# Attention, PReLU layer and soft MoE on one core: the reciprocal of `den` spread by DMA, a later hold of the divided rows, larger K and V rings, and a last stage with block transposes and unread products

## Chip, cores and metric

One NeuronCore of a Trainium2 chip. The metric is the device time of one execution in microseconds (us), lower is better.

## What is computed

```python
def phi(x):
    proj = np.einsum('bhsd,df->bhsf', x, w_phi)
    proj = proj - np.max(np.abs(proj), axis=-1, keepdims=True)
    return np.concatenate([np.exp(proj), np.exp(-proj)], axis=-1)
q_p, k_p = (phi(q), phi(k))                      # q, k, v: 8 batches, 8 heads, 576 tokens, 64
kv = np.einsum('bhsf,bhsd->bhfd', k_p, v)
z = np.sum(k_p, axis=2)
num = np.einsum('bhsf,bhfd->bhsd', q_p, kv)
den = np.einsum('bhsf,bhf->bhs', q_p, z)[..., None] + 1e-06
x = num / den                                    # as 4608 tokens x 512
h = x @ w_in                                     # 512 x 2048
x = (np.maximum(h, 0) + alpha * np.minimum(h, 0)) @ w_out
logits = x @ phi                                 # soft MoE: 8 experts x 4 slots
slot_input = softmax_over_tokens(logits).T @ x   # 32 x 512
slot_out[e] = np.maximum(slot_input[e] @ w1[e], 0) @ w2[e]
out = softmax_over_slots(logits) @ slot_out
```

## The kernel before

**Tiling.** The 4608 tokens are cut into 12 blocks of 384 (`n`), and the 2048 hidden features into 16 chunks of 128 (`c`). One pair (n, c) is a slot: `gemm` (line 498 of the kernel before) makes 12 products of 128 x 384 into the bank `ph` (line 505; `x` and `w_in` are each held as a high and a low fp32r part, and the low-by-low term is left out). `leaky` (510) applies the PReLU on ACT and DVE into `gT`, `turn_g` (528) transposes `gT` in 32 x 32 blocks on DVE and makes products for the logits (`pl`, 540), and per block `softmax` (549) weighs the tokens and adds their sum (`pS`, line 602) into `acc`. `w_out` is applied only to that 32-row sum, in the last stage.

**Attention in the same program.** `k_pair` makes `kv` and `z` for a pair of heads, `q_pair` (382) projects, exponentiates and makes `num` (435) and `den` (442) for a pair of heads and one block, and `q_finish` (453) ends a block: `den` has four groups of 32 rows, one for each sign and head of a pair; a product with the constant `densum` adds the two signs and spreads each sum over 16 rows (460), DVE takes the reciprocal (464), ACT and DVE split it into two fp32r parts `rhl` (469, 470), and for each of the four pairs two products with the constant `densel` spread it over 64 rows a head (`sel`, 477 and 478). DVE multiplies `num` with `sel` (484), ACT rounds it to `xhi` (485), and DVE takes the rest `xlo` (486). `xhi` and `xlo` have one buffer each: those of block n can be written when the last `ph` of block n-1 has read its own.

**Order.** Every step is put by hand at a slot and a phase of it (`at(slot, "pre" | "pe" | "pe2" | "post", ...)`), and a timeline scheduler then sets each engine's order; an engine runs its instructions in that order. All DMAs of the kernel go through the one queue of SP, in order, and each waits there for its buffer. Two blocks (`VB`) bring back deferred `gT` from DRAM in `reload`.

**Last stage.** Behind the last `ph` come the softmax of block 11, its `pS`, four adds into `acc`, then transposes and products with `w_out` (`pg` 757, `px` 762), `sT`, the experts' first layer (`pe`, 782) with transposes `pth` on PE (790), the second layer (`pso`, 819), between which nine groups of four transposes `pc` (808) turn the combine weights into `cT`, and then for each half of the 512 columns (`dh`) the output: 36 products `po` (836) of 128 x 256 fp32r, copied out by ACT and DVE (841, 839) into three rotating tiles `os`, and 9 DMAs of 512 KB (842). The weights `w_out`, `w1`, `w2` come by DMA as 144 pieces of 256 KB (`fetch`) into buffers as these fall free. `spin` (105) issues products that nobody reads (`SPIN` says how many at each place).

Of the kernel before, what the change touches and what calls it, by code (L numbers as in the profile page):

```python
# [28 lines left out]
TB = BT // 128  # L29
NT = T // 128  # L30
E = 8
# [3 lines left out]
KVB = 6  # L35
# [8 lines left out]
SPIN = [5, 3, 13, 6]  # L44

F64_LEAST = struct.unpack("<f", struct.pack("<I", 0x38100000))[0]
# [15 lines left out]
def attention_prelu_softmoe(ctx: ExitStack, tc, qT, kT, v, wphi, w_in, w_out, alpha, phi, w1, w2, out):  # L62
# [10 lines left out]
    gT_d = dram.tile([NDEF, NC, 128, BT], F32, name="gT_d")  # L73

# [27 lines left out]
    def spin(count, before):  # L102
        turn = bank("spin", ps_d)
# [28 lines left out]
    eps_den = const.tile([128, 1], F32, name="eps_den")  # L132
    densum = att.tile([128, 128], F32, name="densum")
    densel = xp.tile([128, NP, 128], F32R, tag="densel", name="densel")

    wpr = sm.tile([128, NC, NSL], F32, tag="wpr", name="wpr")
    acc = const.tile([128, 4, 512], F32, name="acc")
# [5 lines left out]
    def setup_a():  # L143
        nc.vector.memset(ones, 1.0)
        nc.vector.memset(eps_den, 0.0)
        nc.vector.memset(eps_den[0:32], 1e-6)
        nc.vector.memset(eps_den[64:96], 1e-6)

    def setup_b():
# [8 lines left out]
        for p in range(NP):  # L158
            for j in range(2):
                a, b = 64 * j + p, 64 * j + 32 + p  # L160
                r = 32 * p + 16 * j
                nc.vector.tensor_tensor(
                    out=densum[:, r:r + 16], in0=ident[:, a:a + 1].to_broadcast([128, 16]),
                    in1=ident[:, b:b + 1].to_broadcast([128, 16]), op=ALU.add)
                nc.vector.tensor_copy(densel[:, p, 64 * j:64 * j + 64], ident[:, r:r + 1].to_broadcast([128, 64]))

    sched = {}

# [14 lines left out]
    def conv(slot, src, use):  # L183
# [21 lines left out]
        def second():  # L205
# [3 lines left out]
            nc.vector.tensor_tensor(out=w, in0=m, in1=st["sign"], op=ALU.mult)  # L209
# [172 lines left out]
    def q_pair(slot, n, p, late=0):  # L382
# [34 lines left out]
        def feature():  # L417
            pj, mb = st["pj"], st["mb"]
            nc.vector.tensor_tensor(out=pj, in0=pj, in1=mb, op=ALU.subtract)  # L419
            tags = ("qa0", "vg0", "qa1", "vg1") if n == 0 else ("qa0",) * 4  # L420
            st["e", 0] = (attk.tile([128, 4, BT], F32, tag=tags[p], name="qe")[:, 0:2] if tags[p][0] == "v"
# [5 lines left out]
        def attend():  # L427
# [25 lines left out]
    def q_finish(slot, n):  # L453
        st = q_st[n]

        def sums():
            rd = st["rd"] = sm.tile([128, BT], F32, tag="dT", name="rd")
            nc.scalar.activation(rd, st["den"][:, 0:BT], AF.Identity, bias=eps_den)
            ps = st["ps"] = bank("densum")
            nc.tensor.matmul(ps[:, 0:BT], densum, rd, start=True, stop=True)  # L460
# [5 lines left out]
        def split():  # L466
            rhl = xp.tile([128, 2, BT], F32R, tag="rhl", name="rhl")
            rhi, rlo = st["rhi"], st["rlo"] = rhl[:, 0], rhl[:, 1]
            nc.scalar.copy(rhi, st["rc"])
            nc.vector.tensor_tensor(out=rlo, in0=st["rc"], in1=rhi, op=ALU.subtract)  # L470
            xhi_t[n] = xp.tile([128, KD, BT], F32R, tag="xhi", name="xhi")
            xlo_t[n] = xp.tile([128, KD, BT], F32R, tag="xlo", name="xlo")

        def spread(p):
            def go():
                ps = st["sel", p] = bank("sel")
                nc.tensor.matmul(ps[:, 0:BT], densel[:, p, :], st["rhi"], start=True, stop=False)  # L477
                nc.tensor.matmul(ps[:, 0:BT], densel[:, p, :], st["rlo"], start=False, stop=True)
            return go

        def scale(p):
            def go():
                xs = st["num"][:, p, :]
                nc.vector.tensor_tensor(out=xs, in0=st["sel", p][:, 0:BT], in1=xs, op=ALU.mult)
# [4 lines left out]
        at(slot, "pe", sums)  # L489
        at(slot, "post", recip)  # L490
        at(slot + 1, "pre", split)
        for p in range(NP):
            at(slot + 1, "post", spread(p))
            at(slot + 1, "post", scale(p))
# [27 lines left out]
    def reload(n, c):  # L522
        gT4 = attk.tile([128, 4, BT], F32, tag=f"vg{c // 4 % 2}", name="gT4")
# [374 lines left out]
```

## Time and profile before

| what | us |
|---|---|
| three runs | 1056.34, 1056.88, 1061.24 (median 1056.88) |
| the profiled execution, its own time | 1057.16 |
| its span, first to last instruction | 1055.4 |
| PE busy / DVE busy / ACT busy / POOL busy | 984.1 / 773.8 / 469.8 / 149.2 |
| DMA: moved, mean rate | 110.60 MB, 105 GB/s |

A busy PE is not PE at its peak: products are pipelined, and their ends are modelled. The engines' shares are means over stages with different limits, so the profile is read by stages: up to about 234 us the conversion of `w_in` and `w_out` and the attention of the first blocks fill DVE, from 259 to 954.5 us `ph` runs without a break, and from 954.5 us on the last stage.

### The profile page before, as it was taken

What the parts mean: (1) busy time and instruction counts of PE and PEld (TensorE: products, weight loads), DVE (VectorE), ACT (ScalarE), POOL (GpSimd) and SP (SyncE); (2) the same over time, 40 slices, a digit from 0 to 9 for tenths busy, and PEclk for the clock granted to TensorE, in tenths of its full rate; (3) what the DMA queues carried; (4) which work ended last, traced back from release to release, by engine and by line L of the source; (5) the groups of instructions that cost most, each with busy time, mean ns of one, the idle gap of its engine ahead of it and who ended that gap; (6) DMA issues with size and microseconds to landing.
All of it is one profiled execution on the core that took longest, in us unless ns stands there. A gap on an engine that the chain in (4) does not pass through costs nothing.

```text
span 1055.4 us, 21864 instructions
## 1 busy us (share of the span) xinstructions
PE 984.1 (93%) x9038; PEld 685.2 (65%) x9038; DVE 773.8 (73%) x1552; ACT 469.8 (45%) x908; POOL 149.2 (14%) x88
## 2 busy tenths in 40 slices
PE   3787998998999999999999999999999999998994
PEld 1445776774676776676666776767667767787353
DVE  3999989879767578587878687687888486874133
ACT  3876867776444245144235344343334343200133
POOL 2201214121111212121112111121112221000000
PEclk7898999998999999999999999999999999999995
DMA  5343653653010111010401111110401200769879
GB/s 199 120 141 125 193 188 114 225 178 100 9 31 31 39 31 38 20 51 19 163 10 38 32 39 31 31 38 19 160 19 46 96 8 2 249 226 327 261 235 309
DMA packets 71986, 110.60 MB, mean 105 GB/s; under 512 B 7248, under 2 KB 47312, under 8 KB 71888
## 3 DMA queue, kind: packets, MB, share of 16 engines
q1 hardware_dynamic: 71888, 109.22, 32.0%
q8 instruction: 71, 1.16, 0.4%
q14 instruction: 27, 0.22, 0.1%
HBM read 89.27 MB, written 19.92 MB: 103 GB/s over the span
## 4 chain that ended last, share of the span: by engine, by line
PE 71%; DVE 3%; DMA 2%; ACT 1%; issue 1%; DVEq 0%; ACTq 0%; SPq 0%
PE ph L505 34%; PE num L435 5%; PE pS L602 5%; PE pkv L333 5%; PE pl L540 4%; PE den L442 3%; PE pq L403 3%; PE pk L289 2%; DMA out_dram<-os 2%; PE pso L819 1%; PE pe L782 1%; PE sel L477 1%; PE pt L355 1%; PE pr L558 1%; PE densum L460 1%; PE pkv L339 1%
## 5 line engine op out<-in xcount | busy, mean ns | idle before, releaser
L505 PE MATMUL ph<-xhi,w 128*128 128x384 f32 x1536 | 435.2, 351 | 6.5 <-DVE gT L515 4.4
L505 PEld LDWEIGHTS ph<-xhi,w 128*128 128x128 f32 x1536 | 279.0, 189 | 76.8 <-issue 41.5
L505 PE MATMUL ph<-xlo,w 128*128 128x384 f32 x768 | 255.1, 340 | 0.0
L415 POOL PARTITION_ALL_REDUCE mb<-pj x48 | 140.4, 2928 | 553.0 <-ACT pj L409 450.1
L505 PEld LDWEIGHTS ph<-xlo,w 128*128 128x128 f32 x768 | 143.6, 188 | 12.6 <-issue 6.1
L515 DVE SCALAR_TENSOR_TENSOR gT<-gT,alpha_neg,ph 128x384 f32<-128x384 f32 x104 | 62.9, 605 | 77.3 <-ACT ph L514 76.5
L532 DVE STREAM_TRANSPOSE gb<-gT 128x384 f32<-128x384 f32 x192 | 105.6, 566 | 5.7 <-DMA gT<-gT_d 1.9
L513 ACT ACTIVATE gT<-ph 128x384 f32<-128x384 f32 x104 | 50.8, 489 | 114.8 <-PE ph L505 114.0
L425 ACT ACTIVATE qe<-pj 128x768 f32<-128x768 f32 x92 | 73.9, 839 | 59.5 <-DVE pj L419 56.2
L517 DVE TENSOR_SCALAR gT<-ph,alpha_sb 128x384 f32<-128x384 f32 x88 | 53.8, 613 | 46.2 <-PE ph L505 45.8
L333 PE MATMUL pkv<-kp,vt 128*64 128x256 f32 (+1 forms) x640 | 85.0, 400 | 1.1 <-DVE wpr L250 1.1
L435 PE MATMUL num<-qe,kv 128*64 128x192 f32 (+1 forms) x496 | 70.9, 417 | 0.0
L283 ACT ACTIVATE kp<-kp 128x512 f32<-128x512 f32 (+1 forms) x80 | 46.8, 586 | 51.6 <-DVE kp L282 51.1
L333 PEld LDWEIGHTS pkv<-kp,vt 128*64 128x64 f32 (+1 forms) x640 | 41.3, 140 | 39.4 <-issue 17.1
L280 DVE TENSOR_REDUCE mx<-pk 128x4 f32<-128x512 f32 (+1 forms) x80 | 50.2, 627 | 11.4 <-PE pk L289 9.7
L602 PE MATMUL pS<-gb,d 32*32 32x256 f32 x2304 | 55.0, 385 | 0.3 <-DVE logits L594 0.2
L403 PE MATMUL pq<-qraw,wp 64*128 64x384 f32 x192 | 48.9, 562 | 6.7 <-DMA qraw<-in_qT_dram 4.1
L446 ACT COPY num<-num 128x384 f32<-128x384 f32 x48 | 22.8, 475 | 67.1 <-PE num L435 64.2
L409 ACT COPY pj<-pq 128x768 f32<-128x768 f32 x44 | 35.2, 799 | 36.3 <-PE pq L403 36.3
L419 DVE TENSOR_TENSOR pj<-pj,mb 128x768 f32<-128x768 f32 x48 | 46.6, 971 | 6.0 <-POOL mb L415 6.0
L282 DVE TENSOR_TENSOR kp<-pk,mx 128x512 f32<-128x512 f32 (+1 forms) x80 | 50.2, 627 | 0.8 <-PE pkv L333 0.2
L514 ACT ACTIVATE ph<-ph 128x384 f32<-128x384 f32 x104 | 50.6, 487 | 0.0
(191 smaller groups left out, 1345.6 us busy)
## 6 DMA issues: line engine op xcount, KB each, us to landing
w<-in_w_dram SPq DMA_DIRECT2D x58, 256.0 KB, 5.7
qraw<-in_qT_dram SPq DMA_DIRECT2D x48, 192.0 KB, 2.4
out_dram<-os SPq DMA_DIRECT2D x18, 512.0 KB, 3.7
raw<-in_w_in_dram SPq DMA_DIRECT2D x16, 512.0 KB, 3.6
raw<-in_w_out_dram SPq DMA_DIRECT2D x16, 512.0 KB, 4.2
gT_d<-gT SPq DMA_DIRECT2D x32, 192.0 KB, 2.0
gT<-gT_d SPq DMA_DIRECT2D x8, 768.0 KB, 5.2
pf<-in_w_dram SPq DMA_DIRECT2D x21, 256.0 KB, 6.0
```

Source lines behind the costliest of these rows:

```text
L333: return lambda: nc.tensor.matmul(pkv[64 * j:64 * j + 64, 0:256], vt[:, 64 * j:64 * j + 64], feats(t, j).rearrange("p s f -> p (s f)"), st ...
L403: lambda j=j, sl=slice(64 * j, 64 * j + 64): nc.tensor.matmul(pq[j][:, 0:BT], wp[sl], st["qraw"][sl], start=True, stop=True)
L415: nc.gpsimd.partition_all_reduce(mb, pj, 128, bass_isa.ReduceOp.absmax)
L425: nc.scalar.activation(st["e", s], pj, AF.Exp, scale=(1.0, -1.0)[s])
L435: lambda s=s, j=j: nc.tensor.matmul(num[64 * j:64 * j + 64, o:o + w], kvs[:, s, 64 * j:64 * j + 64], st["e", s][:, j, o:o + w], start=(s = ...
L505: gemm_last[0] = nc.tensor.matmul(h, (w_in_hi, w_in_lo)[a][c][:, 128 * k:128 * k + 128], (xhi, xlo)[b][:, k, :], start=(i == 0), stop=(i = ...
L513: nc.scalar.activation(gT, h, AF.Relu, scale=-1.0)
L514: nc.scalar.activation(h, h, AF.Relu)
L515: nc.vector.scalar_tensor_tensor(out=gT, in0=gT, scalar=alpha_neg[:, c:c + 1], in1=h, op0=ALU.mult, op1=ALU.add)
L517: nc.vector.tensor_scalar(out=gT, in0=h, scalar1=0.0, scalar2=alpha_sb[:, c:c + 1], op0=ALU.min, op1=ALU.mult)
L532: nc.vector.transpose(out=gb[n, c // 8][:, c % 8, :], in_=gT)
L602: lambda j=j, i=i, h=h: nc.tensor.matmul(pS[i][32 * (j % 4):32 * (j % 4) + 32, 256 * h:256 * h + 256], st["d"][32 * i:32 * i + 32, 32 * j: ...
```

## The change

- **Reciprocal by DMA.** `den` is laid out so that the two signs add up in the bank (384 columns as two halves of 192 on other rows). DVE adds 1e-6 and takes the reciprocal of 192 columns, two DMAs write it to DRAM (`rc_d`) and two read it back spread over 64 rows each (`bc`, 128 x 4 x 384). `densum`, `densel`, `rhl`, `sel` and their products are gone.
- **Later hold.** The block's end moves to slot 16(n-1)+7, the multiplication with `bc` (`divide`) and the split (`scale`) to six slots later; the multiplication is held on DVE behind the PReLU of that slot (`mark`). The pairs of Q stand 3 slots apart, not 4.
- **Rings.** `KVB`, the buffers of `kv` and `zt`, 6 to 8; `gT` comes back in 2 chunks a DMA with three buffers, not in 4 with two.
- **Last stage.** The sum in `acc` is carried by products (`carry`, `pa`), the four row groups are added in the bank; `pg` is four whole transposes; the experts' hidden rows and the combine weights are transposed in 32 x 32 blocks on DVE, so `pth` and `pc` are gone; `w2` is loaded with another row order; `po` becomes a pair of fp32 products of 32 rows each that use different row groups and banks; behind each pair stand three unread products into `idle`; `os` has nine tiles; more unread products stand between the other steps.

```diff
-KVB = 6
+KVB = 8
-SPIN = [5, 3, 13, 6]
+SPIN = [5, 3, 8, 3, 8, 5, 5, 5, 3]
...
-            for b, o, w in segments(n):
-                kvs, zt = kv_t[NP * b + p]
+            for s in (1, 0):
                 together([
-                    lambda g=g: nc.tensor.matmul(
-                        den[32 * g:32 * g + 32, o:o + w], zt[:, g, :], st["e", g % 2][:, g // 2, o:o + w],
-                        start=(p == 0 and o == 0), stop=(p == NP - 1 and o + w == BT))
-                    for g in (3, 1, 2, 0)])
+                    lambda j=j, h=h, zt=kv_t[NP * ((n * BT + h * HB) // S) + p][1]: nc.tensor.matmul(
+                        den[64 * j + 32 * h:64 * j + 32 * h + 32, 0:HB], zt[:, 2 * j + s, :],
+                        st["e", s][:, j, HB * h:HB * h + HB],
+                        start=(p == 0 and s == 1), stop=(p == NP - 1 and s == 0))
+                    for j in (1, 0) for h in (1, 0)])
...
         def recip():
-            rc = st["rc"] = sm.tile([128, BT], F32, tag="dT", name="rc")
-            nc.vector.reciprocal(out=rc, in_=st["ps"][:, 0:BT])
...
-                nc.tensor.matmul(ps[:, 0:BT], densel[:, p, :], st["rhi"], start=True, stop=False)
-                nc.tensor.matmul(ps[:, 0:BT], densel[:, p, :], st["rlo"], start=False, stop=True)
...
+            rd = sm.tile([128, BT], F32, tag="dT", name="rd")[:, 0:HB]
+            nc.vector.tensor_scalar(out=rd, in0=st["den"][:, 0:HB], scalar1=1e-6, scalar2=None, op0=ALU.add)
+            nc.vector.reciprocal(out=rd, in_=rd)
+            for j in range(2):
+                nc.sync.dma_start(rc_d[n % 2][j].rearrange("p h t -> h p t"), rd[64 * j:64 * j + 64])
+        def widen():
+            bc = st["bc"] = xp.tile([128, NP, BT], F32, tag="bc", name="bc")
+            for j in range(2):
+                nc.sync.dma_start(
+                    bc[64 * j:64 * j + 64], rc_d[n % 2][j, 0:NP].rearrange("p h t -> p (h t)").unsqueeze(0).to_broadcast([64, NP, BT]))
...
+                ins = nc.vector.tensor_tensor(out=xs, in0=st["bc"][:, p, :], in1=xs, op=ALU.mult).ins
+                tc.add_manual_dep(ins, mark[max(k for k in mark if k <= slot + 6)].name, nosync, reason="behind the load")
...
-                q_pair(NC * (n - 1) + 4 * p + -6 + (-1 if n == 1 else 0), n, p)
-        q_finish(-39 + 18 + 5 if n == 0 else NC * (n - 1) + -6 + 12 + 5 + (-1 if n == 1 else 0), n)
+                q_pair(NC * (n - 1) + 3 * p - 6 - (p > 0 or n == 1), n, p)
+        q_finish(-39 + 18 + 5 if n == 0 else NC * (n - 1) + 7, n)
...
+            spun[0] = spin(SPIN[3], together([
+                lambda i=i: nc.tensor.matmul(pa[32 * i:32 * i + 32, :], tsc, acc[i], start=True, stop=False)
+                for i in (3, 2, 1, 0)], spun[0]))
+            gather()
...
+                last[dh] = spin(SPIN[8], together([
+                    lambda j=j, r=2 * h + j, sl=slice(64 * h + 32 * j, 64 * h + 32 * j + 32): nc.tensor.matmul(
+                        po[j][:, 0:256], logits[sl, 4 * i:4 * i + 4, :].rearrange("p t s -> p (t s)"), sor[sl], start=True, stop=True)
+                    for j in range(2)], last.get(dh)), idle)
```

Where the block's end moved, PE's order at the start of block 6 (`w_1268` and `w_1259` hold the last chunk's weights of block 5, `w_637` and `w_633` the first chunk's of block 6). Before:

```order
L289 MATMUL pk<-wp,kraw 128x128 x8
L505 MATMUL ph<-xhi,w_1268 128x384
L477 MATMUL sel<-rhl,densel 128x384 x2
L478 MATMUL sel<-rhl,densel 128x384 x2
L477 MATMUL sel<-rhl,densel 128x384
L478 MATMUL sel<-rhl,densel 128x384
L442 MATMUL den<-qe,zt 32x192 x8
L477 MATMUL sel<-rhl,densel 128x384
L478 MATMUL sel<-rhl,densel 128x384
L505 MATMUL ph<-xhi,w_637 128x384 x4
L540 MATMUL pl<-gT,wpr 32x384 x4
```

And with the change:

```order
L345 MATMUL pt<-ident,kvT 128x128 x3
L492 MATMUL ph<-xhi,w_1259 128x384 x2
L492 MATMUL ph<-xlo,w_1259 128x384
L492 MATMUL ph<-xhi,w_1259 128x384
L393 MATMUL pq<-qraw,wp 128x384 x2
L492 MATMUL ph<-xhi,w_633 128x384 x6
L528 MATMUL pl<-gT,wpr 32x384 x4
L492 MATMUL ph<-xhi,w_662 128x384
```

The eight `sel` products that stood between the two blocks' `ph` are gone, and so is the `den` of the next block among them; a projection `pq` stands there now.

In the last stage, PE around the output (`w_...` hold `w2`). Before:

```order
L825 MATMUL prp<-so,tident 128x256
L819 MATMUL pso<-w_10242,hTm 32x256 x3
L819 MATMUL pso<-w_10245,hTm 32x256 x4
L819 MATMUL pso<-w_10248,hTm 32x256 x4
L819 MATMUL pso<-w_10251,hTm 32x256 x4
L819 MATMUL pso<-w_10254,hTm 32x256 x4
L836 MATMUL po<-sor,cT 128x256 x36
L825 MATMUL prp<-so,tident 128x256
L836 MATMUL po<-sor,cT 128x256 x36
```

And with the change:

```order
L822 MATMUL prp<-so,tident 128x256
L816 MATMUL pso<-num,acc_111 32x256 x3
L816 MATMUL pso<-bc,acc_111 32x256 x6
L816 MATMUL pso<-w_10212,acc_111 32x256 x4
L816 MATMUL pso<-w_10215,acc_112 32x256 x4
L816 MATMUL pso<-w_10218,acc_112 32x256 x3
L834 MATMUL po<-sor,logits 128x256 x2
L108 MATMUL idle<-ident 128x128 x3
```

The last two rows follow one another 18 times; then come the 25 `pso` that are left, `prp`, and again 18 times a pair of `po` and three unread products. The output of the first half so stands ahead of a part of the second half's `pso`.

## Rows read from the trace of the kernel before

**Rows 1.** The page, its first line.

```profile
span 1055.4 us, 21864 instructions
```

**Rows 2.** Windows by stage: us; PE, PEld, DVE, ACT, POOL busy; PEclk; DMA share; GB/s.

```profile
234.00:259.00 25.00, 19.20 (x149) 10.45 (x147) 23.51 (x46) 15.31 (x31) 2.32 (x1) 0.86 0.32 96
...
329.00:954.50 625.50, 617.02 (x5926) 440.45 (x5923) 471.00 (x919) 235.28 (x451) 88.81 (x48) 1.00 0.19 63
954.50:983.00 28.50, 24.16 (x329) 16.98 (x331) 8.82 (x25) 3.81 (x14) 0.95 (x1) 0.88 0.83 270
...
1000.70:1022.80 22.10, 22.10 (x300) 11.92 (x299) 7.46 (x39) 5.78 (x11) 0.00 (x0) 1.00 0.79 251
1022.80:1055.40 32.60, 16.99 (x74) 13.32 (x74) 13.63 (x21) 10.73 (x19) 0.00 (x0) 0.66 0.87 290
```

**Rows 3.** Chain of waits, one stretch of dense `ph` products: start us, length us.

```profile
938.72 8.55 PE ph L505 x48
```

**Rows 4.** Groups of instructions by shape, PE; busy us, mean ns, idle before.

```profile
L477 PE MATMUL sel<-rhl,densel 128*128 128x384 f32 x48 | 18.2, 401 | 8.0 <-DVE num L484 5.6 <-ACT rhl L469 2.4
...
L478 PE MATMUL sel<-rhl,densel 128*128 128x384 f32 x48 | 16.2, 372 | 1.9 <-DVE rhl L470 1.9
...
L460 PE MATMUL densum<-rd,densum 128*128 128x384 f32 x24 | 10.4, 513 | 0.0
```

**Rows 5.** Timeline of PE at the start of block 6; idle before in brackets.

```profile
549.00 0.60 PE L477 MATMUL sel<-rhl,densel 128*128 128x384 f32 x2
549.92 0.62 PE L478 MATMUL sel<-rhl,densel 128*128 128x384 f32 x2 [0.32 <-DVE rhl L470]
552.38 0.69 PE L477 MATMUL sel<-rhl,densel 128*128 128x384 f32 x1 [1.84 <-DVE num L484]
...
553.32 1.51 PE L442 MATMUL den<-qe,zt 128*32 128x192 f32 x16
...
555.57 0.94 PE L505 MATMUL ph<-xhi,w 128*128 128x384 f32 x4
...
557.22 0.45 PE L505 MATMUL ph<-xhi,w 128*128 128x384 f32 x1
```

**Rows 6.** Chain of waits, last stage.

```profile
961.97 3.99 PE pS L602 x173
...
976.30 5.02 PE px L762 x32
...
983.02 1.85 PE pe L782 x16
...
987.41 3.57 PE pe L782 x32
...
1006.05 0.57 PE pso L819 x8
...
1007.21 1.86 PE pso L819 x32
```

**Rows 7.** Timeline, last stage: unread products; output issues; last output copy.

```profile
958.13 3.06 PE L105 MATMUL spin<-ident 128*128 128x128 f32 x26
...
1024.25 26.85 SPq L842 DMA_DIRECT2D out_dram<-os  x18
...
1049.97 0.69 DVE L839 COPY os<-po 128x512 f32<-128x512 f32 x1 [0.95 <-DMA out_dram<-os]
```

**Rows 8.** Timeline of PE, one row-tiled pair and the product behind it.

```profile
541.94 0.92 PE L403 MATMUL pq<-qraw,wp 64*128 64x384 f32 x4
542.78 0.45 PE L505 MATMUL ph<-xhi,w 128*128 128x384 f32 x1
```

**Rows 9.** DMA issues: count, KB each, median us to landing.

```profile
gT_d<-gT SPq DMA_DIRECT2D x32, 192.0 KB, 2.0
...
vt<-in_v_dram SPq DMA_DIRECT2D x16, 320.0 KB, 3.2
```

**Rows 10.** Waits of the DMA queue SP: total us, times, longest.

```profile
SPq L391 <- PE pq L403: 224.4, 33, 22.3
```

More of the change, by code (lines that the diff above doesn't have):

```diff
@@ L73, in attention_prelu_softmoe @@
     gT_d = dram.tile([NDEF, NC, 128, BT], F32, name="gT_d")
+    rc_d = [dram.tile([2, 32, 2, HB], F32, name=f"rc_d{i}") for i in range(2)]
     const = ctx.enter_context(tc.tile_pool(name="const", bufs=1))
@@ L100, in together, with spin @@
         return before
-    def spin(count, before):
-        turn = bank("spin", ps_d)
+    def spin(count, before, turn=None):
+        turn = turn or bank("spin", ps_d)
         return together([
@@ L157, in setup_b @@
             nc.vector.tensor_tensor(out=o, in0=o, in1=ident[:, 96:128], op=ALU.add)
[L158 to L165, printed above, removed]
     sched = {}
+    mark = {}
     after = [NC * (b + 1) + VR for b in VB]
@@ L546, in attention_prelu_softmoe @@
     first = [True]
[L547 removed]
+    gemm_last, spun, last = [None], [None], {}
     def softmax(step, n):
@@ L606, in gather @@
             if n == NB - 1:
-                spun[0] = spin(SPIN[3], last)
+                spun[0] = spin(SPIN[4], end)
         def add():
@@ L715, in attention_prelu_softmoe @@
                 fetch(attk, tag)
-            for tag in ("vg0", "vg1"):
-                fetch(attk, tag, 3)
+            for i in range(3):
+                fetch(attk, "vg", 1, 3)
             for i in range(KPB):
                 fetch(attk, "kp2", 2, KPB)
-        if slot == 170:
+        if slot == 168:
             close_pool("attq")
@@ L772, in attention_prelu_softmoe @@
-    hTm = [attk.tile([128, 4, E, NSL], F32, tag="kp2", name="hTm", bufs=KPB) for f in range(2)]
-    for t in hTm:
-        nc.gpsimd.memset(t, 0.0)
-    hrs = attk.tile([128, 2, 512], F32, tag="kp2", name="hrs", bufs=KPB)
-    hr_t = {}
-    for eg in range(2):
+    pa = last["pa"]
+    spun[0] = spin(SPIN[5], together([
+        lambda i=i: nc.tensor.matmul(pa[32 * i:32 * i + 32, :], tident[:, 0:32], acc[i], start=False, stop=True)
+        for i in range(4)], spun[0]))
+    half = [slice(0, 256), slice(256, 512)]
@@ new lines, in attention_prelu_softmoe @@
+    nc.scalar.copy(acc[0][:, half[0]], pa[:, half[0]])
+    nc.vector.tensor_copy(acc[1][:, half[1]], pa[:, half[1]])
+    pg, px, psi = bank("pg"), bank("px"), bank("psi")
+    spun[0] = spin(SPIN[6], together([
+        lambda c=c: nc.tensor.transpose(pg[:, 128 * c:128 * c + 128], acc[c // 2][:, 128 * c:128 * c + 128], ident)
+        for c in range(4)], spun[0]))
+    nc.scalar.copy(aT[:, half[0]], pg[:, half[0]])
+    nc.vector.tensor_copy(aT[:, half[1]], pg[:, half[1]])
+    spun[0] = spin(SPIN[7], together([
+        lambda i=i, c=c: nc.tensor.matmul(
+            px[32 * c:32 * c + 32, :], aT[:, 128 * c + 32 * i:128 * c + 32 * i + 32], got["wo", 4 * i + c], start=(i == 0), stop=(i == 3))
+        for i in range(4) for c in range(4)], spun[0]))
@@ new lines, in attention_prelu_softmoe @@
+    nc.scalar.activation(acc[2][:, half[0]], px[:, half[0]], AF.Identity, scale=lsum)
+    nc.vector.tensor_scalar(out=acc[3][:, half[1]], in0=px[:, half[1]], scalar1=lsum, scalar2=None, op0=ALU.mult)
+    for k in range(KD):
+        nc.tensor.matmul(psi[:, 32 * k:32 * k + 32], acc[2 + k // 2][:, 128 * k:128 * k + 128], tident[:, 0:32], start=True, stop=True)
+    nc.scalar.copy(sT, psi[:, 0:KD * NSL].rearrange("p (k s) -> p k s", k=KD))
+    own = sm.tile([128, 8], F32, tag="sc", name="own", bufs=2)
@@ new lines, in attention_prelu_softmoe @@
+    for eg in range(2):
+        for j in range(4):
+            nc.vector.tensor_reduce(
+                out=own[:, j:j + 1], in_=ident[:, 36 * j + 16 * eg:36 * j + 16 * eg + 4], axis=AX.X, op=ALU.add)
+        nc.vector.tensor_reduce(out=own[:, 4 + eg:5 + eg], in_=own[:, 0:4], axis=AX.X, op=ALU.add)
+    nc.vector.tensor_scalar(out=own[:, 4:6], in0=own[:, 4:6], scalar1=F32_MOST, scalar2=None, op0=ALU.mult)
+    hT = []
+    for eg in range(2):
+        hr = attk.tile([128, EF], F32, tag="kp2", name="hr", bufs=KPB)
@@ L813, in attention_prelu_softmoe @@
-    so2 = pf.tile([128, 2, 256], F32, tag="pf12", name="so")
-    sor2 = pf.tile([128, 2, 256], F32R, tag="pf13", name="sor")
+            nc.vector.tensor_scalar(
+                out=hr[:, 512 * fh:512 * fh + 512], in0=pe, scalar1=0.0, scalar2=own[:, 4 + eg:5 + eg], op0=ALU.max, op1=ALU.min)
+        t = acc[2 * eg:2 * eg + 2]
+        for b in range(2):
+            nc.vector.transpose(
+                out=t[b].rearrange("p (b s) -> p b s", s=32),
+                in_=hr.rearrange("p (f b) -> p b f", b=32)[:, 16 * b:16 * b + 16])
```

201 lines of the change are left out of this document (79 added, 122 removed).

## The prediction

> **What bounds the kernel now.** I read the page first, then the windows by stage, the groups of PE, the timeline of a block's start, and last the chain of the final stage. The span is 1055.4 us [rows 1]; the profiled execution took 1057.16 us, 1.8 us more, and 0.28 us above the median of the runs. I count from 1057.2.
>
> The windows [rows 2] show three regimes. From 329 to 954.5 us PE is busy 617 of 625.5 us at the full clock (1.00 is 2.4 GHz; a figure below it is a mean over stretches at this level and at 1.2 GHz) while DVE has 471 us of work: PE's order sets the pace, and what leaves PE there leaves the time. Between 234 and 259 us it is otherwise: DVE is busy 23.5 of 25 us, PE 19.2, and the granted clock is 0.86; the `ph` of block 2 have to wait for the end of its attention. In the last stage two things alternate. From 1000.7 to 1022.8 us PE is busy throughout, from 1022.8 us on only 17.0 of 32.6 us, at a clock of 0.66, with the DMA engines at 0.87 and 290 GB/s: there the output's transfers are the bound. Eighteen issues of 512 KB go out in 26.85 us, 1.49 us for one tile [rows 7].
>
> **Reciprocal by DMA, on PE.** For each block eight `sel` and one `densum` product go; the new `den` has as many columns in as many passes as the old, and costs what it cost. A dense `ph`, of the same 128 x 384 fp32r shape as `sel`, takes 8.55 / 48 = 0.178 us [rows 3]; `densum`, fp32, has two records of 0.51 us that overlap in part, 10.4 / 12 = 0.87 us for one block [rows 4]. By pace that is 8 x 0.178 + 0.87 = 2.3 us a block, 25 us for the eleven blocks behind the first. But the products also stand in a chain: PE waited 8.0 us before the first and 1.9 us before the second kind of `sel` [rows 4]. Block 6 is the plainest: from the first `sel` at 549.0 us to the dense `ph` at 557.22 us pass 8.2 us [rows 5], in which `sel` have 1.4 us of work; PE waits 0.32 us for the split and 1.84 us for the multiplication on DVE. The new order has no product that waits for DVE there; a rest stays, since `xhi` has one buffer and its first part is cast on ACT only when the old block's last product has read it. Lower end: pace alone with `densum` at one record, (1.42 + 0.51) x 9 blocks behind 329 us = 17 us. Upper end: all that the groups show, 18.2 + 16.2 + 10.4 + 9.9 = 55 us. I take the pace of eleven blocks and half of the waits, **-30 us**, near the pace, because the busy time of a group holds waits that other products may fill.
>
> **The same on DVE, ACT and SP.** DVE loses half of each reciprocal and the split, and its product with `bc` stays; it has 155 us to spare behind 329 us [rows 2], so this counts nothing there. If it fails to hide, the next to be late is the PReLU, and with it `gT` and PE. New are four DMAs a block on SP. The nearest rows are a write of 192 KB, landed 2.0 us after its issue, and a load of 320 KB in 3.2 us [rows 9]; `bc` is two of 384 KB, so the way there and back takes about 2.0 + 3.5 to 4.5 = 6 us. The order puts the product with `bc` behind the reciprocal by one to eight slots of 12 `ph` (seven of the eleven blocks five or more, block 9 four, block 10 two, blocks 1 and 7 one), and a slot of dense `ph` alone is 2.1 us. In the tight blocks DVE would stand for some 2 us; PE has work for that time, as `xhi` is needed only at the block's end. I count 0; upper end 3 blocks x 4 us = 12 us.
>
> **Block 2 and the rings.** The Q pairs end four slots sooner and the end of a block too; DVE's order now has 25 PReLUs ahead of block 2's reciprocal where it had 32, and its `w_out` conversions come later, beside `ph`. The 25 us from 234 to 259 us hold 19.2 us of PE work at a reduced clock, with DVE full. Ends: nothing is gained (DVE's work remains and must be done before the steady stretch), or all but the 5.8 us that PE idles plus the clock's loss, 25 x 0.14 = 3.5 us, and as much again at the two starts before it: 19 us. I take **-8 us**, near the middle. The larger rings of K and V and the three buffers of `gT` free loads sooner; nothing in the stretch where PE is full waits long for them, so 0.
>
> **The last stage up to the output.** Priced from its own rows [rows 6, 7]. An unread product costs 3.06 / 13 = 0.235 us (26 records are 13 products). A pass of four products of 512 columns side by side is 3.57 / 4 = 0.89 us, from `pe`; one of 256 columns 1.86 / 4 = 0.465 us, from `pso`.
> - From the last `ph` (954.5) to `pS` (961.97): 7.5 us, unchanged.
> - `pa`, one pass, and three unread products: 0.9 + 0.7. Then `pS`, 4.0.
> - Eight unread products, which cover the copies: 1.9. The closing `pa` 0.9, five unread 1.2, four transposes 0.6, five unread 1.2, `px` four passes 3.6 (5.02 before, partly at half clock), five unread 1.2, `psi` and its copy 0.8.
> Sum 24.5: `pe` starts near 979.0 instead of 983.0. `pe` takes 4 x 3.57 = 14.3 without the transposes `pth` and `psi` between, so it ends near 993.3 instead of 1000.7. The 128 `pso` take 14.9, the two `prp` with the copies round them 3.0. That is 11 us gained ahead of the output, and the loads of `w2` keep up: 46 pieces behind `px` at some 0.75 us each (256 KB at the output's rate) end by about 1012 us.
>
> **The output itself.** Here the change works against itself. 36 pairs of `po` come with 108 unread products, in PE's own order, so they are paid whether the output waits for DMA or not. The trace has no fp32 pair of 32 rows by 256 columns. The nearest row is `pq`, a pair of 64 rows and 384 columns between full-array products: the next product begins 0.84 us behind it [rows 8], and 0.84 x 256 / 384 = 0.56 us. With three unread products 0.56 + 0.71 = 1.27 us a pair, 2.5 us a tile, against 1.49 us for its DMA. Thirty-six pairs take 45.7 us. So: 993.3 + 14.9 + 3.0 + 45.7 = 1056.9, less the last three unread products, plus the last copy 0.4 and, as before, 4.7 us from the last copy's end (1050.66) to the span's end: about 1061.3, **+6 us** against 1055.4. Lower end: the unread products cost nothing and DMA bounds the output, 18 x 1.49 = 27 us behind the last load, 1044 us, -11. Upper end: the pair's two products do not run side by side, 36 x 0.465 = 17 us more, +23.
>
> On the price of a pair, rows and a page can be set against each other. A visit of `pso` among transposes, x8, takes 0.57 us where the dense rows give 0.465 [rows 6]: some 0.1 us is lost by going to and fro. The Trainium skill (TensorEngine Tiling (Array Packing), Key Properties) says that a change of the tiling mode drains TensorE; the pairs and the unread full-array products change it 72 times. By that rule, with the trace agreeing in the 0.1 us, the `pq` price holds; without it the dense price would give 36 x (0.465 + 0.71) = 42.3 us, 3.4 less.
>
> **Sum.** -30 - 8 + 6 = -32: 1057.2 - 32 = 1025 us; against the median 0.3 less, which I let stand.
>
> **Rivals.**
> - The output is bounded by DMA after all and the unread products lie in its shadow: -30 - 8 - 11 gives 1008 us. For it speaks that DMA is the bound there now; against it that 2.5 us of PE work a tile exceed 1.49. Chance 0.13.
> - The pairs do not run side by side: 1025 + 17 = 1042 us. The pairs of `pq` do share a pass, which speaks against it. 0.10.
> - PE gets only the pace back, and block 2 nothing, since DVE, at three quarters busy, becomes late instead: 1057.2 - 17 + 6 = 1046 us. 0.13.
> - Slower: the way through DRAM is late. SP is one queue in order, and loads of Q in it waited 33 times, 224.4 us in all, up to 22.3 us [rows 10]. If the read of `bc` stands behind such a wait in each block, DVE stops at the product with `bc`, the PReLU behind it stops, and `ph` finds no free bank. A mean wait of 6.8 us plus 6 us is 13 us; it decides once it exceeds the distance from reciprocal to product, about 2 to 4 us a slot, so in blocks with three slots or fewer. With 5 us lost at each of eleven blocks, and no gain of waits there, 1057.2 - 20 + 55 + 6 - 8 = 1090 us; at half of them about 1063. The order of SP puts at most a few loads between write and read. 0.07.
> - The unread products don't do what they are for: the clock falls in the output all the same (it was 0.66, rows 2), and 45.7 us of products grow by half or more, 1050 to 1070 us. Against it: PE would be busy without a break. 0.05.
>
> **Numbers.** The forecast has 0.52, with 1012 to 1038 us for itself. The range 1003 to 1046 us reaches over the first three rivals and leaves out the last two and the tails, about 0.2. A measurement of this kernel can tell some 0.5%, 5 us, from no change. Faster by more than that: 0.52 + 0.13 + 0.10 and most of 0.13, 0.86; within it, 0.06; slower, 0.08.
>
> **What would show it.** Right: no PE wait at a block's start longer than about 1 us; block 2's first `ph` well before 258 us; `pe` starting 24 to 25 us behind the last `ph`; the output's pairs at about 1.27 us each with PE full, the clock at full speed, and outgoing DMAs 2.5 us apart, with the stage from the last `ph` to the end some 106 us long (101 before). Wrong: `bc` as the reason of DVE's idle time; output DMAs 1.5 us apart; or a body of the blocks, from `ph` to `ph`, as long as before.

## The result, and the profile after

The changed kernel takes 1071.41 us (median of 4 runs, 1070.07 to 1076.39), the one before beside it 1057.89: ratio 1.0131, interval 1.0100 to 1.0162. It is 1.3% slower; 1025 us, 3% faster, was predicted. The profiled execution took 1070.44 us.

The windows of the changed kernel by stage, columns as in [rows 2]; ahead of them the page's first line:

```profile
span 1068.7 us, 22668 instructions
...
329.00:952.70 623.70, 596.11 (x5951) 431.78 (x5952) 461.81 (x902) 220.05 (x427) 84.64 (x43) 0.98 0.25 73
952.70:980.00 27.30, 24.55 (x351) 16.83 (x353) 9.32 (x36) 4.21 (x11) 0.00 (x0) 0.94 0.95 302
...
1005.90:1068.70 62.80, 57.70 (x412) 39.44 (x412) 15.72 (x37) 13.79 (x37) 0.00 (x0) 0.99 0.54 184
```

The first row answers the second of [rows 2]. PE's busy time fell from 617.0 to 596.1 us, as the products that went away promised, but its idle time rose from 625.5 - 617.0 = 8.5 to 27.6 us and the granted clock fell from 1.00 to 0.98: the last `ph` ends at 952.7 instead of 954.5 us. From there to the end it takes 116.0 us instead of 100.9, with the DMA engines half idle in the output (0.54, before 0.87).

The waits of the changed kernel (engine, line and tile, what it waited for: us in all, times, longest):

```profile
DVE num L472 <- DMA bc<-rc_d: 19.5, 4, 6.7
ACT xhi L465 <- DVE num L472: 19.4, 4, 6.8
...
PE pl L528 <- DMA gT<-gT_d: 12.6, 4, 4.0
...
PE ph L492 <- ACT xhi L465: 10.7, 4, 5.9
```

Two waits are new. In four blocks the product of `num` with `bc` stands for the read of `bc`, and PE behind it for `xhi`; and PE waits for the parked rows `gT`. The chain of waits ahead of block 7 shows the first (start us, length us):

```profile
608.85 0.83 PE den L431 x16
...
611.22 1.23 DVE rd L449
...
612.74 0.28 SPq L451
613.02 0.05 issue
613.07 3.40 DMA rc_d<-rd
616.47 0.02 issue
616.49 4.93 DMA bc<-rc_d
...
621.51 1.96 DVE num L472 x4
```

From the first issue to the landing of `bc` pass 621.42 - 612.74 = 8.7 us; I had taken 6. It lands as the last `ph` of block 6 ends (621.4 us); PE has a `pq` and three `pt` left to do there and then waits 1.48 us for `xhi`. The longest wait, 5.9 us, is block 1's.

The chain in the last stage, as in [rows 6]:

```profile
979.95 13.94 PE pe L799 x128
993.89 9.06 PE pso L816 x166
1002.95 0.63 PE prp L822 x2
1003.58 2.30 PE pso L816 x40
1005.87 0.63 PE po L834 x4
1006.50 0.87 PE idle L108 x6
```

The last two rows repeat to the end: a pair 0.63 us, three unread products 0.86, 1.495 us in all, for 36 pairs 53.8 us; 18 output DMAs go out in 56.39 us, 3.1 us apart, where 26.85 us stood before [rows 7].

### The profile page after: what moved, and what is told of

Same layout as the page of the kernel before. It is cut to its first block, busy times and chain, and to the rows that moved or that the text cites. A ratio compares the mean times of both kernels' runs of the same rounds, so it can differ in the third digit from the quotient of the medians.

```text
span 1068.7 us, 22668 instructions
## 1 busy us (share of the span) xinstructions
PE 987.5 (92%) x9428; PEld 698.5 (65%) x9428; DVE 761.6 (71%) x1509; ACT 448.1 (42%) x883; POOL 145.7 (14%) x86
## 4 chain that ended last, share of the span: by engine, by line
PE 73%; DVE 13%; DMA 6%; ACT 4%; issue 3%; SPq 0%; POOL 0%; DVEq 0%; ACTq 0%; POOLq 0%
PE ph L492 34%; PE pkv L323 6%; PE num L425 5%; PE pS L591 4%; PE pl L528 3%; PE den L431 3%; PE idle L108 3%; PE pq L393 3%; PE po L834 2%; PE pk L279 2%; DMA bc<-rc_d 2%; DMA gT<-gT_d 2%; DMA rc_d<-rd 2%; PE pso L816 1%; PE pe L799 1%
## 5 line engine op out<-in xcount | busy, mean ns | idle before, releaser
L492 PE MATMUL ph<-xhi,w 128*128 128x384 f32 x1536 | 435.5, 353 | 20.3 <-ACT xhi L465 10.7
L492 PEld LDWEIGHTS ph<-xhi,w 128*128 128x128 f32 x1536 | 283.1, 192 | 82.9 <-issue 37.7
L492 PE MATMUL ph<-xlo,w 128*128 128x384 f32 x768 | 260.1, 345 | 1.8 <-DVE xlo L466 1.8
L492 PEld LDWEIGHTS ph<-xlo,w 128*128 128x128 f32 x768 | 146.0, 191 | 14.3 <-issue 6.6
L323 PE MATMUL pkv<-kp,vt 128*64 128x256 f32 (+1 forms) x640 | 87.4, 409 | 1.4 <-ACT kp L274 1.4
L270 DVE TENSOR_REDUCE mx<-pk 128x4 f32<-128x512 f32 (+1 forms) x80 | 50.0, 625 | 15.3 <-PE pk L279 12.0
L528 PE MATMUL pl<-gT,wpr 128*32 128x384 f32 x384 | 42.8, 521 | 14.6 <-DMA gT<-gT_d 12.6
L279 PE MATMUL pk<-wp,kraw 64*128 64x128 f32 x512 | 39.4, 296 | 14.1 <-issue 10.5
```

Source lines behind the costliest of these rows:

```text
L279: lambda t=t, j=j, sl=slice(64 * j, 64 * j + 64): nc.tensor.matmul(st["pk"][:, j, F * t:F * t + F], st["kraw"][sl, 128 * t:128 * t + 128], ...
L323: return lambda: nc.tensor.matmul(pkv[64 * j:64 * j + 64, 0:256], vt[:, 64 * j:64 * j + 64], feats(t, j).rearrange("p s f -> p (s f)"), st ...
L492: gemm_last[0] = nc.tensor.matmul(h, (w_in_hi, w_in_lo)[a][c][:, 128 * k:128 * k + 128], (xhi, xlo)[b][:, k, :], start=(i == 0), stop=(i = ...
L528: lambda g=g: nc.tensor.matmul(pl_t[n][32 * g:32 * g + 32, :], wpr[:, c - 3 + g, :], gT_t.pop((n, c - 3 + g)), start=(c == 3), stop=(c == ...
```

## Experiments

Each edit is against the kernel that is named with it; where none is, against the changed one. Where the span went is read from three pieces of each profile, in us: the end of block 2's last `ph`; from there to the last `ph`; from there to the end of the span.

| kernel | median | block 2 ends | then to the last `ph` | then to the end |
|---|---|---|---|---|
| before | 1057.9 | 328.6 | 626.0 | 100.9 |
| changed | 1071.4 | 325.0 | 627.7 | 116.0 |
| tail_alone | 1072.7 | 328.3 | 629.6 | 114.1 |
| front_alone | 1062.8 | 322.4 | 634.9 | 103.7 |
| no_unread | 1045.4 | 323.0 | 628.3 | 91.2 |
| unread1 | 1064.6 | 323.4 | 629.2 | 116.7 |
| tail_no_unread | 1046.5 | 327.2 | 626.2 | 88.7 |
| rc_prev | 1026.1 | 317.6 | 617.6 | 89.7 |
| k_early | 1033.5 | 334.5 | 608.7 | 89.5 |
| k_e3 | 1035.6 | 337.5 | 609.2 | 87.5 |
| kv6 | 1045.6 | 325.2 | 629.3 | 90.9 |
| ring4 | 1038.0 | 324.4 | 621.8 | 90.6 |
| kr6 | 1027.8 | 328.4 | 607.3 | 90.1 |
| spread4 | 1029.3 | 330.5 | 607.4 | 90.2 |
| gt2_act | 1042.3 | 323.7 | 625.2 | 90.9 |
| gt_act | 1026.0 | 330.8 | 602.7 | 90.0 |
| gt_pool | 1033.3 | 330.2 | 609.3 | 92.4 |

### Which half is slow

**tail_alone**: the kernel before with the new last stage.

```diff
-SPIN = [5, 3, 13, 6]
+SPIN = [5, 3, 8, 3, 8, 5, 5, 5, 3]
...
+        if n == NB - 1:
+            at_step(step + 2, "pe2", carry)
```

> The kernel before with the new last stage alone (reciprocal, hold, Q spacing and rings as before). Theory M (the last stage itself costs 15 us: from the last ph to the end 101 us before, 116 us in the changed kernel; what precedes it is another matter): before + 15, about 1073 us. Rival (the last stage is long only because of what the front part hands it, loads or clock): before, 1058 us, or less by the 4 us that pe starts earlier.

Measured 1072.69 us, ratio 1.0134 (1.0103 to 1.0165). **front_alone**: the changed kernel with the old last stage.

```diff
-SPIN = [5, 3, 8, 3, 8, 5, 5, 5, 3]
+SPIN = [5, 3, 13, 6]
...
-            at_step(step + 2, "pe2", carry)
```

> The changed kernel with the old last stage. Theory M (the 25 us of PE work that left are eaten by new waits of PE, 44.7 us idle between the first and the last ph against 19.0): within 3 us of before, 1055 to 1058 us. Rival (the front part is a gain of some 20 us, which the last stage's 15 us and something between them hide): about 1040 us.

Measured 1062.76 us, ratio 1.0044 (1.0024 to 1.0064). So the last stage alone costs the whole loss, and the front, where I looked for 38 us, gives nothing; tail_no_unread and no_unread below, which differ by the front alone, lie 1 us apart.

### The output

**no_unread**: nothing between the pairs.

```diff
-SPIN = [5, 3, 8, 3, 8, 5, 5, 5, 3]
+SPIN = [5, 3, 8, 3, 8, 5, 5, 5, 0]
```

> The changed kernel without the three unread products behind each pair of the output (SPIN's last entry 0). Theory M (they are paid in PE's order, 36 x 0.865 = 31 us, and hold back what DMA could send at 1.5 us a tile): output bounded by DMA from about 1010 us on, 27 us + 5, a span near 1044 us, time near 1047 us, 24 us less than the changed kernel. Rival (without them the clock falls to half and the pairs take 1.2 us or more each): span near 1058 us, time near 1060 us. Second rival (they cost nothing, DMA bounds the output anyway): 1071 us.

Measured 1045.4 us, ratio 0.9875 (0.9850 to 0.9899). The stage shrinks from 116.0 to 91.2 us, and the output is bounded by its DMAs again; the windows, and the queue of SP (17 of the 18 output DMAs, as the row begins at 1010 us; 26.21 / 17 = 1.54 us each):

```profile
1004.90:1029.00 24.10, 21.97 (x179) 11.60 (x177) 11.21 (x30) 9.72 (x30) 0.00 (x0) 1.00 0.92 309
1029.00:1042.40 13.40, 2.91 (x25) 1.68 (x22) 2.70 (x8) 2.22 (x7) 0.00 (x0) 0.72 0.91 302
```

```profile
1009.86 26.21 SPq L839 DMA_DIRECT2D out_dram<-os  x17
```

The clock, which the unread products were to hold, stays at 1.00 through the pairs without them: the last pair ends at 1032.5 us, and the 0.72 of the second window comes from what lies behind it. **unread1**: one in place of three (the last number of `SPIN` is 1).

> The changed kernel with one unread product behind each pair of the output instead of three. If what the three cost is PE's own time, 0.288 us each in the trace of after: 36 pairs take 10 us more than in no_unread, of which the outgoing DMAs hide the part in the first half of the output: 1050 to 1056 us. Rival (one keeps the clock up to the end and costs nothing behind the DMAs): 1043 to 1046 us.

Measured 1064.6 us, 1058.78 to 1074.23: above both ranges. The nine runs fall into two groups: five at 1058.8 to 1064.6 us with a mean granted clock of 0.967 to 0.975, four at 1069.7 to 1074.2 us with 0.949 to 0.962. The profile is of one of the four (1071.0 us). The two halves of the output in the windows, and the chain over the edge between them:

```profile
1005.00:1036.30 31.30, 30.84 (x189) 15.57 (x178) 8.92 (x21) 7.82 (x21) 0.00 (x0) 1.00 0.66 222
1036.30:1069.20 32.90, 28.80 (x92) 15.39 (x92) 6.79 (x16) 5.97 (x16) 0.00 (x0) 0.50 0.42 144
```

```profile
1034.57 0.63 PE po L834 x4
1035.20 0.42 PE idle L108 x2
...
1036.90 1.15 PE po L834 x4
1038.06 0.73 PE idle L108 x2
```

At the full clock a pair with one unread product takes 1.05 us; from 1036.3 us on the granted clock is 0.50, the lower level, and it takes 1.88. In this run one unread product was thus followed by a stretch at half clock; in the five shorter runs it was presumably shorter or absent, which no profile shows. In the changed kernel's profile, with three for 16 us more of PE's own time, it does not come, and in no_unread, with none, it does not come either. The first unread product behind a pair takes 0.42 us, each further one (0.86 - 0.42) / 2 = 0.22. The Trainium skill (TensorEngine Tiling (Array Packing), Key Properties) says that a change of the tiling mode drains TensorE; the 0.2 us that the first one takes more agree.

**tail_no_unread**: tail_alone with the last number of `SPIN` 0.

> The kernel before with the new last stage alone, and no unread products in its output. If the last stage's price is independent of the front (tail_alone was 14.7 us over before, leaving the unread products out was worth 26.0 in the whole change): 1044 to 1049 us, 36 pairs limited by the outgoing DMAs at over 300 GB/s. Rival (without them the clock falls early in the output, as in the last stage of before): 1052 us or more.

Measured 1046.47 us, ratio 0.9894 (0.9878 to 0.9911), 26.2 below tail_alone, as no_unread is 26.0 below the changed kernel: the output's price doesn't depend on the front.

### The reciprocal's way

**rc_prev**, against no_unread:

```diff
-nc.sync.dma_start(rc_d[n % 2][j].rearrange("p h t -> h p t"), rd[64 * j:64 * j + 64])
+nc.sync.dma_start(rc_d[0 if n == 0 else 1][j].rearrange("p h t -> h p t"), rd[64 * j:64 * j + 64])
...
-bc[64 * j:64 * j + 64], rc_d[n % 2][j, 0:NP]
+bc[64 * j:64 * j + 64], rc_d[0][j, 0:NP]
```

> The changed kernel with no unread products in the output (1045.4 us); each block reads block 0's reciprocals back from DRAM instead of its own, which it still writes, to a row that nobody reads. The computation left out: every block but the first is divided by the sums of block 0. The same bytes move and the read still stands behind the write in SP's queue, but it does not wait for the write to land. Theory T (the way to DRAM and back is late at blocks 1, 7 and 10, 4 waits of PE with 9.2 us and 19 us of DVE): the read starts about 3 us sooner, most of these waits go, 1036 to 1041 us. Rival (DVE comes to the product late by its order anyway): 1044 to 1047 us.

Measured 1026.14 us, 19.3 below no_unread, more than either theory gave. The expectation was wrong on one point: the read doesn't stay behind the write. In the trace it goes out as soon as `bc` is free, for block 7 at 516.4 us, while that block's own write comes at 598.2. So the division no longer waits for its own `den` and reciprocal either, and 19.3 us is an upper end for the way through DRAM. PE's waits for `xhi` shrink from 9.2 us to 0.6; the rest is waits for `gT` (13.2 to 8.4 us) and less time at half clock. Behind block 2 the gain is 10.7 us (628.3 to 617.6).

Why is the way late in some blocks? In the trace of no_unread `den` of blocks 7 and 10 ends 12 and 10 us ahead of the old block's last `ph` (block 1: 6 us), in blocks 2 to 6, 8, 9 and 11 it is 21 to 48. Both reach into a new sequence, and what comes last there is that sequence's K pair: the last Q pair of a block was moved four slots forward, the K pairs that they read were not. Block 4 reaches into a new sequence too and has 27 us; 7 and 10 come two blocks after a parked block's rows (in blocks 5 and 8), and whether that sets them apart no run tells. **k_early**, against no_unread:

```diff
-k_pair(int(-40 + 2.5 * i) if i < 4 else int(-20 + 6 * (i - 4)) if i < 8 else 6 * i - 42, i)
+k_pair(int(-40 + 2.5 * i) if i < 4 else int(-20 + 6 * (i - 4)) if i < 8 else 6 * i - 46, i)
```

> The changed kernel with no unread products in the output (1045.4 us), and each K and v pair from the ninth on asked for four slots sooner, as the change did with the q pairs; nothing else. In the order of PE the last den of blocks 7 and 10, whose rows reach into a new sequence, then stands after the eighth chunk of the block before instead of the thirteenth; block 1 stays where it is. Theory K (the q pairs were moved four slots forward and the K pairs that they read were not, so that the way to DRAM and back is late at the blocks that cross into a new sequence): the waits of DVE for bc at blocks 7 and 10 (4.4 and 4.8 us) and PE's wait for xhi there go, the parked rows' reloads come behind bc instead of beside it: 1032 to 1038 us. Rival (the trip itself is too long, wherever it starts, or the parked rows hold the time): 1043 to 1047 us.

Measured 1033.49 us, ratio 0.9772 (0.9744 to 0.9799). Of the waits these rows are left:

```profile
PE pl L528 <- DMA gT<-gT_d: 10.1, 4, 4.3
DVE num L472 <- DMA bc<-rc_d: 9.5, 2, 6.5
```

The two waits left for `bc` are at blocks 0 and 1; PE's wait for `xhi` is 0.8 us. In block 1, though, PE's wait has only changed its name: it waits for a `kp` that stands on DVE behind the late multiplication.

```profile
163.45 0.56 DVE L472 TENSOR_TENSOR num<-bc,num 128x384 f32<-128x384 f32 x1 [6.50 <-DMA bc<-rc_d]
163.93 0.68 DVE L272 TENSOR_TENSOR kp<-pk,mx 128x512 f32<-128x512 f32 x1
...
164.76 1.65 PE L393 MATMUL pq<-qraw,wp 64*128 64x384 f32 x4 [6.65 <-DVE kp L272]
```

Behind block 2 it gains 628.3 - 608.7 = 19.6 us: PE idles 9.1 us less there (27.9 to 18.8) and is busy 10.5 less, as the clock falls less often (0.98 to 0.99) and as the work of one K pair now lies ahead of block 2's end. That work is paid there: PE's busy time ahead of it rises by 6.6 us, DVE's by 11.2 (262.8 to 274.0), and block 2 ends 11.5 us later, for DVE has no room for it. What the edit is worth is the 11.9 us of the whole. **k_e3**, against k_early:

```diff
-int(-20 + 6 * (i - 4)) if i < 8
+int(-20 + 5 * (i - 4)) if i < 8
```

> As k_early, and the fifth to eighth K pairs, which block 1 reads, at every fifth slot instead of every sixth: the last den of block 1 comes after the thirteenth chunk of block 0 instead of the fifteenth, that of block 2 after the eighth of block 1 instead of the tenth. Theory K: block 1's wait (5.3 us of DVE, 7.9 us of PE between 157.2 and 165.1 us) goes too, 5 to 8 us below k_early. Rival (DVE is what block 0 waits for, and earlier K pairs push the conversion of the weights back): within 2 us of k_early or above it.

Measured 1035.63 us, a miss: DVE's wait in block 1 falls only from 6.5 to 4.8 us, and though PE now idles there 1.2 us instead of 6.7, block 2 ends 3 us later still.

### The parked rows and the rings

**kv6**, against no_unread:

```diff
-KVB = 8
+KVB = 6
```

> The changed kernel with no unread products in the output (1045.4 us), and with the K and v rings at 6 as before; nothing else. If the larger rings are worth the 8 us that I gave them: 1051 to 1055 us, block 2 ends 8 us later than the 323.0 us of no_unread. Rival (they only move the gap ahead of block 2 into its first ph's, as 264.6 to 291.2 us in the trace): 1043 to 1048 us, block 2 ends within 2 us of it.

Measured 1045.6 us: the larger K and v rings give nothing. The changed kernel with all rings as before (rings_back) has no time, as its buffers need 0.375 KB a partition more than the core's SBUF memory has; ring4 therefore has one buffer of weights fewer. **ring4**, against kv6 (in short):

```diff
-PF = 14
+PF = 13
...
-        gT2 = attk.tile([128, 2, BT], F32, tag="vg", name="gT2", bufs=3)
+        gT4 = attk.tile([128, 4, BT], F32, tag=f"vg{c // 4 % 2}", name="gT4")
```

> The changed kernel with no unread products in the output (as in no_unread, 1045.4 us) and with the buffers of before for the parked rows: gT comes back four chunks at a time into two buffers, eight chunks asked for ahead, instead of two at a time into three buffers, six ahead; K and v rings of 6 instead of 8, which pays for it, and one buffer fewer for weights of the last stage. Theory W (the smaller ring of gT took back the gain): the 13.2 us in which PE waits for gT<-gT_d go, and with them the half clock behind them (10 us of it at 505 to 516 and 748 to 755, worth about 5 us), less what the smaller K ring costs: 1023 to 1033 us, no wait of PE for gT over 1 us in the two virtual blocks. Rival S (the wait is only where the block's slack falls; another wait on DVE or ACT takes its place): 1040 to 1047 us.

Measured 1037.95 us, between the theories: 7.6 below kv6, but PE's waits for `gT` are not shorter (15.3 us, kv6 12.3). The gain lies in blocks 6, 7 and 9 (3.4, 2.8 and 4.0 us from last `ph` to last `ph`; block 8 takes 2.8 longer), right after the blocks in which the parked rows come back; why there, no run tells. **kr6** is ring4 with the K pairs of k_e3 (both edits above).

> As k_e3, with the K and v rings back at 6 and the parked rows' buffers back at two of four chunks (as in ring4, one buffer fewer for weights of the last stage). If the smaller gT ring costs what ring4 showed against kv6 (7.6 us) whatever the reciprocals do: 7 us below k_e3. If it only cost because the reloads stood beside a late bc: within 2 us of k_e3. In both, rings of 6 hold the K pairs at their earlier places; were they needed, this is 5 us or more above k_e3.

Measured 1027.77 us, ratio 0.9722 (0.9696 to 0.9748). It is 7.9 below k_e3, as the first theory said, but not for its reason: block 2 ends 9 us sooner, the stretch behind it is 2 us shorter, the last stage 2.6 longer, and PE's waits for `gT` are still 11.5 us. With early K pairs the old rings of K, v and `gT` together are the better ones; no run separates them there. Its queue of SP in the first parked block, and PE there (idle before, in brackets):

```profile
501.53 1.13 SPq L451 DMA_DIRECT2D rc_d<-rd  x2
504.45 1.63 SPq L456 DMA_DIRECT2D bc<-rc_d  x2
506.13 1.04 SPq L264 DMA_DIRECT2D vt<-in_v_dram  x2
507.27 9.70 SPq L512 DMA_DIRECT2D gT<-gT_d  x3
```

```profile
501.18 1.47 PE L528 MATMUL pl<-gT,wpr 128*32 128x384 f32 x16
...
514.61 1.51 PE L528 MATMUL pl<-gT,wpr 128*32 128x384 f32 x8 [5.47 <-DMA gT<-gT_d]
```

PE has read the old rows at 502.6 us; the reload goes out at 507.3, behind the write and the read of the reciprocals and two loads of v. In the kernel before no such DMAs stand there: PE reads its old rows from 510.4 us on, and the reload goes out at 511.3. **spread4**, against kr6, tries more distance instead:

```diff
-at_step(s0 + c // 4, "virtual", lambda m=m, c=c: [turn_g(m, c + j) for j in range(4)])
+at_step(s0 + [0, 1, 5, 6][c // 4], "virtual", lambda m=m, c=c: [turn_g(m, c + j) for j in range(4)])
```

> As kr6 (1027.8 us), with the four steps in which a parked block's rows are turned and multiplied at places 0, 1, 5 and 6 of its ten instead of 0 to 3, and its softmax three places later; nothing else. If PE's waits for gT<-gT_d (11.5 us in kr6, in two spells, each with 6.8 us of half clock behind it) are the time that two reloads of four chunks need from their issue to their landing, four steps between hide them: 1014 to 1021 us. Rival (all ten places hold little other work for PE, so that it waits the same at another name): 1025 to 1030 us.

Measured 1029.27 us, the wait 12.3 us: the rival. **gt_act**, against kr6, and **gt2_act**, the same against no_unread:

```diff
-        nc.sync.dma_start(gT4, gT_d[n, c:c + 4].rearrange("c p t -> p c t"))
+        nc.scalar.dma_start(gT4, gT_d[n, c:c + 4].rearrange("c p t -> p c t"))
```

> As kr6 (1027.8 us), with the parked rows' reloads issued from ACT's queue instead of SP's; nothing else. Theory Q (in kr6 the reload's buffer is free at 502.6 us and it is issued at 507.3, behind two writes of the reciprocals that wait for DVE and two reads that wait for the writes, and lands at 514.6): issued 4 to 5 us sooner, PE's wait for gT<-gT_d falls from 11.5 to 3 to 6 us and with it some of the 13.6 us of half clock: 1018 to 1024 us. Rival (the reload's own way, 5 to 7 us, or the 384 KB of bc ahead of it, hold it wherever it is issued): 1026 to 1030 us.

> The changed kernel with no unread products in the output (1045.4 us), its three buffers of two chunks and its rings of 8 as they are, and the parked rows' reloads issued from ACT's queue. If the queue and not the size of the ring is what makes PE wait for gT: 13.2 us of waits fall to under 6, 1036 to 1041 us. Rival (three small buffers can't hide a reload whoever issues it): 1043 to 1047 us.

Measured 1025.95 us, ratio 0.9700 (0.9679 to 0.9721), and 1042.25 us, ratio 0.9855 (0.9835 to 0.9875): both between their theory and the rival, and no more than 1.8 and 3.1 us below kr6 and no_unread, whose intervals they overlap. The waits are clearer than the times. The queues of ACT and of SP in gt_act:

```profile
504.29 1.16 ACTq L512 DMA_DIRECT2D gT<-gT_d  x2
```

```profile
503.72 1.13 SPq L451 DMA_DIRECT2D rc_d<-rd  x2
507.60 6.30 SPq L456 DMA_DIRECT2D bc<-rc_d  x2
```

The reload goes out as soon as its rows are read, and the waits fall from 11.5 to 7.6 and from 13.2 to 7.9 us. So the queue is the cause of a third and more of them; behind block 2 the gain is 4.6 us in gt_act, 3.9 of it in block 5, where the first parked rows come back, and 3.1 us in gt2_act; gt_act loses 2.4 ahead of block 2's end. What is left bears out the rival: in gt_act the second reload is issued at 504.93 us, and PE waits for it until 515.43. The Trainium skill (Trainium Kernel Development and Optimization, Key Constraints) says that issuing DMAs from several engines only saves the sequencer's issue time; here it also took a reload out from behind two waits. **gt_pool** has `nc.gpsimd.dma_start` in that place.

> As gt_act, with the reloads issued from POOL's queue. Theory Q: as gt_act, 1018 to 1024 us, unless POOL's own order (the zeroing of zt, which waits for the products of den) holds the reload, which its issue in the trace would show. Rival as there.

Measured 1033.28 us, PE's wait 14.0 us: above both ranges. POOL's first reload goes out at 503.9, the second only at 510.45 us, when DVE already works on the first (from 510.16 us): the two come one after the other. Slower than from SP.

## Why the prediction was wrong

**The sum.** Forecast -30 - 8 + 6. Measured: the last stage +15 (tail_alone 1072.7 against 1058.0), the front +5 (front_alone) or, in the changed kernel itself, 2 us less up to the last `ph`.

**"-30 us" for the reciprocal on PE.** The pace was right, the waits were not. PE's busy time from 329 us to the last `ph` fell by 20.9 us; nine blocks by 2.3 us are 20.7. But the changed kernel gave it back: its idle time there rose by 19.1 us, and its clock fell. Once most of the new waits are gone (kr6), the stretch behind block 2 is 607.3 instead of 626.0 us, 18.7 less, and 23.3 less in gt_act, both with a K pair's work moved out of it. With the division freed from its own sums the whole front is worth 1046.5 - 1026.1 = 20.4 us (tail_no_unread against rc_prev). No run shows the half of the `sel` waits that I added on top.

**"The way there and back takes about 6 us ... I count 0; upper end 12."** This step failed worst. I had named the tight blocks (1, 7, 10) and the wait of DVE, and both came; I took it for harmless, because PE had other work and `xhi` is needed only at the block's end. But in a tight block the reciprocal starts just there. The way takes 8.7 us, and with the division freed of it 19.3 us come back (rc_prev, an upper end), through three doors: PE's wait for `xhi`, less time at half clock, and the reloads that stand in the same queue. The cause in blocks 7 and 10 is in the diff: Q pairs were moved, K pairs not (k_early takes both waits away). Block 1 needed other steps: there k_early only renames PE's wait, and in k_e3 and kr6 it is 1.2 us and less. The rival "the way through DRAM is late" named the right symptom in three or four blocks, not eleven, but not the cause: in block 7 the read went out 0.02 us after the write had landed, with no other load between them in SP's order, and what PE waited for was `xhi`, not a free bank.

**"The larger rings ... nothing waits long for them, so 0."** Right for K and v (kv6). Wrong for `gT`: PE waits 12.6 us where it waited none. The old size of the ring alone doesn't shorten that (ring4). What stands ahead in SP's order, the reciprocals' DMAs, makes a third and more of it (gt_act, gt2_act); the rest stays open.

**"-8 us" for block 2.** It ends 3.6 us sooner in the changed kernel, and 3 to 6 us sooner in front_alone, no_unread, unread1 and kv6, which have its front: about half. In kr6, with a K pair's work more ahead of it, it ends at the old time. DVE bounds that stretch: 11.2 us more work on DVE made its end 11.5 us later (k_early).

**The last stage, "+6".** Up to the output the terms nearly held: `pe` starts 27.2 us behind the last `ph` (24.5 forecast) and takes 13.94 us (14.3). The mis-sized term is "1.27 us a pair": 0.63 + 0.86 = 1.495, for 36 pairs 8 us more. The mechanism, PE bound by its own unread products while the DMAs idle, was forecast; that the stage would be slower was too, but by 15 us and not by 6. The unread price came from rows without a change of tiling mode [rows 7].

**The signs named ahead** told it at once: `bc` as the reason of DVE's idle time, PE waits over 1 us at a block's start, and a body as long as before.

## What to carry to other kernels

When a step is moved forward, list what it reads and check that those steps moved too; the loss shows only where a block needs the newest of them. A DMA that waits for a result held everything behind it in its queue: try transfers that the critical engine waits for on another queue (here this shortened the waits by 4 to 5 us, the time by less). Unread products between products that bound the stage cost their full time, so time the kernel without them first; what those in the other places give, no run here tests.

The best kernel of these runs, gt_act, takes 1025.95 us (1025.31 to 1029.46), not clearly less than kr6 (1027.57 to 1029.29): the new last stage without unread products in the output, the reciprocal by DMA, K pairs moved forward with the Q pairs, rings of 6 and the reloads on ACT's queue.

## What was not expected of the hardware

- With one unread product between the pairs the granted clock fell to 0.50 at 1036.3 us, though PE had been busy 30.84 of 31.3 us before; with three, and with none in no_unread, it stayed at 1.00 over the pairs. In kr6, with none, it fell in the middle of the output, at 1005.4 us, and stayed there to the end at no cost: 90.1 us from the last `ph` to the end, and 90.0 in gt_act, where the clock was 1.00 through the pairs. The DMAs bounded that stage (share 0.92 from 1005.4 us on). What decides between them no run shows.
- A write of 48 KB is followed by the read that waits for it only after 3.4 us, as long as the parked rows of 192 KB take to land (3.2 us); the read, spread over 64 rows twice, takes 4.9.
- front_alone is 7 us slower behind block 2 than the changed kernel, whose front it has. PE idles as long there (28.6 and 27.6 us), but is busy 606.3 us instead of 600.1, at a granted clock of 0.97 instead of 0.98: the clock makes most of the difference, and why it fell more often no run tells.
- Still open: what would shorten the 7.6 us that PE waits for `gT` in gt_act.
